# Decode attention on one core: softmax moved into the head's own loop body, hardware loops on VectorE and ScalarE, x on ScalarE's queue, wo in 1792-byte rows

## The chip, the cores and the metric

The kernel runs on one core of one Trainium2 chip. The metric is the device time of one execution in microseconds (us), the median of several runs. The *span* is the part of that time that the profile covers, from the first to the last instruction; it is 1.7 to 2.1 us shorter than the device time in most runs here and up to 3.7 us in some, and that small difference will matter. A run is fast or slow in state; all runs that are compared below are fast, except where the text says otherwise (two runs of e6 are slow, and the state of e8's only run is unknown). Differences of under 1% are the subject here, so most kernels were run five times beside the kernel before on the same chip.

## The reference

A decode step of grouped-query attention with a gate. With 4 batches and 8 key/value heads there are 32 heads to stream, each with K and V of 8192 x 256 in bf16, 4.19 MB each. The two query heads of a group share them. A small two-layer MLP gives the gate. Everything else is small beside 32 x 8.4 MB.

```python
B, Sq, D = 4, 1, 448
Hq, Hkv, Sk, Dh = 16, 8, 8192, 256

def _A_ref(x, k_cache, v_cache, wq, wo):
    q = ((x @ wq).reshape(B, Sq, Hq, Dh)).transpose(0, 2, 1, 3)
    k = jnp.repeat(k_cache, 2, axis=1)
    v = jnp.repeat(v_cache, 2, axis=1)
    scores = jnp.einsum("bhqd,bhkd->bhqk", q, k) * (Dh ** -0.5)
    p = _softmax(scores, axis=-1)
    o = jnp.einsum("bhqk,bhkd->bhqd", p, v)
    return o.transpose(0, 2, 1, 3).reshape(B, Sq, Hq * Dh) @ wo

xn = _layernorm(x)
s = _A_ref(xn, k_cache, v_cache, wq, wo)
g = _silu(_B_ref(xn, w1, w2, w3, w4))        # cut: a small MLP
return x + s * g
```

## The kernel before

SyncE issues all the big loads on one queue. K and V have two buffers each; K's is released by PE's count of transposed groups (`p_t`), V's by PE's count of finished PV products (`p_pv`).

```python
def prog_sp(sp):
    sp.dma_start(x_sb[:, :], x2d).then_inc(S["dx"], 16)
    # ... cut: wq, w3, w4, rows of 28,672, 12,544 and 6,272 bytes
    def load_k(h):
        if h >= 2:
            sp.wait_ge(S["p_t"], NGR * (h - 1))
        sp.dma_start(kn_dst(h), ...).then_inc(S["dk%d" % (h % 2)], 16)
    def load_v(h):
        # ... cut: h == 0
            sp.wait_ge(S["p_pv"], h)
        # ... cut: the last V comes in four pieces, dvl0 to dvl3
    load_k(0)
    load_k(1)
    sp.dma_start(wo_sb[:, :, :], A_wo.rearrange("(k p) n -> p k n", p=P)
                 ).then_inc(S["dwo"], 16)          # rows of 896 bytes
    load_v(0)
    for h in range(2, NH):
        load_k(h)
        load_v(h - 1)
    load_v(NH - 1)
```

TensorE (PE) runs a hardware loop over pairs of heads. A head is 16 groups of 8 transposes of K; VectorE or ScalarE evicts each group, and three groups later PE forms its scores. The softmax chain and the PV product *of the previous head* are woven into the groups.

```python
def body(h):
    for j in range(NGR):                       # 16 groups
        f_t(h, j)                              # 8 transposes of K
        if j >= LAG: f_s(h, j - LAG)           # scores, 3 groups behind
        else:        f_s(h - 1, NGR + j - LAG)
        if j == J_RMAX: f_rmaxT(h - 1)         # J = 4, 6, 9
        if j == J_BC:   f_bc(h - 1)
        if j == J_SUM:  f_sum(h - 1)
        if j in PV_SLOTS:                      # groups 10 to 15
            f_pv(h - 1, ...)                   # 128 matmuls in six parts
with nc.Fori(0, NH // 2, engines=[PE], ...):
    body(0); body(1)
# after the loop: last three score groups of the last head, then its softmax
# chain, with the output projection f_o of groups 0 to 6 woven in between,
# then PV by pieces of V, then f_o(7)
```

VectorE and ScalarE are written out in full, head by head, with waits for ever larger semaphore values:

```python
def evac(engine, h, j):
    engine.wait_ge(S["p_t"], NGR * h + j + 1)
    # ... cut: copy pst to kT, on VectorE or on ScalarE

for h in range(NH):                            # unrolled on VectorE
    for j in range(NGR):
        if j in D_GROUPS: evac(v, h, j)
        # ... cut: rmax, diag, negb, rz of head h - 1 at fixed groups
    f_ot(h - 1)                                # psv * rz to OT
```

Of the kernel before, what the change touches and what calls it, by code (L numbers as in the profile page):

```python
# [12 lines left out]
P = 128  # L13
# [19 lines left out]
def bass_recurrent_scan__gqa_block_cached__mixer_s_mlp__decode_kernel(  # L33
# [43 lines left out]
    J_RMAX, J_BC, J_SUM = 4, 6, 9  # L77
    PV_SLOTS = tuple(range(10, 16))
    NPV = NCH * NHALF
    PVW = 32  # L80
# [5 lines left out]
    with ExitStack() as es:  # L86
        def sb(name, shape, dty):
# [5 lines left out]
        wo_sb = sb("wo_sb", [P, NKC, D], BF16)  # L93
# [4 lines left out]
        qc = sb("qc", [P, 2, NHALF, REP], BF16)  # L98
        OT = sb("OT", [P, HKV, REP, NHALF, Bn], BF16)
# [8 lines left out]
        rz = sb("rz", [P, REP], F32)  # L108
# [28 lines left out]
            + ["p_t", "p_sc", "p_m1", "p_m2", "p_m3", "p_pv", "p_x", "p_q", "p_h", "p_h2", "p_o"]  # L137
            + ["v_ev", "a_ev", "v_rmax", "v_diag", "v_neg", "v_ot", "a_exp", "g_q", "g_c",
               "v_xT", "v_qT", "v_hT", "v_bout", "v_c", "v_w", "a_c", "v_out"])}
# [23 lines left out]
        def prog_sp(sp):  # L163
            sp.dma_start(x_sb[:, :], x2d).then_inc(S["dx"], 16)
# [10 lines left out]
            def load_k(h):  # L175
                b, g = divmod(h, HKV)
                if h >= 2:
                    sp.wait_ge(S["p_t"], NGR * (h - 1))
                sp.dma_start(kn_dst(h), A_k_cache[b, g].rearrange("(p c) d -> p (c d)", p=P)
                             ).then_inc(S["dk%d" % (h % 2)], 16)  # L180

            def load_v(h):
                b, g = divmod(h, HKV)
                if h == 0:
                    sp.wait_ge(S["p_h2"], 1)
                else:
                    sp.wait_ge(S["p_pv"], h)
                src = A_v_cache[b, g].rearrange("(p c) d -> p c d", p=P)
                if h < NH - 1:
                    sp.dma_start(vflat[h % 2], src.rearrange("p c d -> p (c d)")  # L190
                                 ).then_inc(S["dv%d" % (h % 2)], 16)
                else:
                    w = NCH // NPIECE
                    for i in range(NPIECE):
                        sp.dma_start(
                            vb[:, h % 2, i * w:(i + 1) * w, :].rearrange("p c d -> p (c d)"),
                            src[:, i * w:(i + 1) * w, :].rearrange("p c d -> p (c d)")
                        ).then_inc(S["dvl%d" % i], 16)
# [3 lines left out]
            sp.dma_start(wo_sb[:, :, :], A_wo.rearrange("(k p) n -> p k n", p=P)  # L202
# [10 lines left out]

        def prog_pool(gp):
            c = _Chain(gp, S["g_c"])
            c(gp.memset(ident_f[:, :], 0.0))
            c(gp.memset(ident_b[:, :], 0.0))
            c(gp.memset(ones_f[:, :], 1.0))
            c(gp.memset(pT[:, :, :].rearrange("p s n -> p (s n)"), 0.0))
            c(gp.memset(vflat[1][:, DK * HDH:NCH * DH], 0.0))  # L220
            c(gp.memset(qc[:, 1].rearrange("p a b -> p (a b)"), 0.0))
            c(gp.memset(kT[:, (NGR - LAG) % RING:RING, :].rearrange("p r n -> p (r n)"), 0.0))
            c.sync()
            for t in (ident_b, ident_f):
                c(gp.affine_select(out=t[:, :], in_=t[:, :], compare_op=ALU.not_equal, fill=1.0,
                                   base=0, pattern=[[-1, P]], channel_multiplier=1))
            gp.wait_ge(S["v_qT"], 1)
            for h in range(NH):
                b, g = divmod(h, HKV)
                if h >= 1:  # L230
                    gp.wait_ge(S["p_sc"], h)
                gp.tensor_copy(qc[:, h % 2], qT[:, b, g]).then_inc(S["g_q"], 1)  # L232

        def evac(engine, h, j):
            engine.wait_ge(S["p_t"], NGR * h + j + 1)
# [7 lines left out]
        def prog_act(act):  # L243
            c = _Chain(act, S["a_c"])
# [8 lines left out]
            def exps(h):  # L253
                s = h % 2
                act.wait_ge(S["v_neg"], h + 2)
                if h >= 1:
                    act.wait_ge(S["p_pv"], h)
# [9 lines left out]
            for h in range(NH):  # L267
                for j in range(NGR):
                    if j not in D_GROUPS:
                        evac(act, h, j)  # L270
                    if j == J_BC:
                        exps(h - 1)
            exps(NH - 1)
# [4 lines left out]
        def prog_dve(v):  # L278
# [34 lines left out]
            c(v.memset(psc[1][:, 0:NCH * REP], 0.0))  # L313
            c.sync()
            v.sem_inc(S["v_ev"], sum(j in D_GROUPS for j in range(NGR - LAG, NGR)))
            v.sem_inc(S["a_ev"], sum(j not in D_GROUPS for j in range(NGR - LAG, NGR)))
            v.sem_inc(S["v_ot"], 1)
            v.sem_inc(S["dv1"], 16)
# [10 lines left out]
            v.wait_ge(S["g_c"], 9)  # L329
# [47 lines left out]
            def f_rmax(h):  # L377
                v.wait_ge(S["p_sc"], h + 2)
# [3 lines left out]
            def f_diag(h):  # L382
                v.wait_ge(S["p_m1"], h + 2)
                c(v.tensor_reduce(gmax[:, :], psm[0:REP, 0:P], AX.X, ALU.max))  # L384
                c.sync()
# [3 lines left out]
            def f_negb(h):  # L389
                v.wait_ge(S["p_m2"], h + 2)  # L390
                v.tensor_copy(negb[:, h % 2, :], psm[:, P:P + REP]).then_inc(S["v_neg"], 1)  # L391

            def f_rz(h):
                v.wait_ge(S["p_m3"], h + 2)
                c(v.reciprocal(rz[:, :], psm[:, P + REP:P + 2 * REP]))

            def f_ot(h):
                b, g = divmod(h % NH, HKV)
                v.wait_ge(S["p_pv"], h + 2)
                c.sync()  # L400
                for dh in range(NHALF):
                    src = psc[0] if (h == NH - 1 and dh == 1) else psv
                    ins = v.tensor_tensor(OT[:, g, :, dh, b], src[:, dh * PVW:dh * PVW + REP],  # L403
                                          rz[:, :], ALU.mult)
                    if dh == NHALF - 1:
                        ins.then_inc(S["v_ot"], 1)
                    else:
                        c(ins)

            for h in range(NH):  # L410
                for j in range(NGR):
                    if j in D_GROUPS:
                        evac(v, h, j)
                    if j == LAG - 1:
                        f_rmax(h - 1)
                    if j == J_RMAX:
                        f_diag(h - 1)
                    if j == J_BC:
                        f_negb(h - 1)
                    if j == J_SUM + 1:  # L420
                        f_rz(h - 1)
                f_ot(h - 1)
            f_rmax(NH - 1)
            f_diag(NH - 1)
            f_negb(NH - 1)
            f_rz(NH - 1)
            f_ot(NH - 1)
# [6 lines left out]
        def prog_pe(pe, xn_mark, xn2_mark):  # L434
            def take(name, n=1):
                pe.wait_ge(S[name], n).then_inc(S[name], -n)  # L436

            pe.wait_ge(S["g_c"], 9)
            for k, (src, mark) in enumerate(((xn_b, xn_mark), (xn2_b, xn2_mark))):
# [6 lines left out]
                if k == 0:  # L446
                    take("v_xT")
            take("dwq", 16)
# [9 lines left out]
            take("dw3", 16)  # L458
            take("v_xT")
# [6 lines left out]
            take("dw4", 16)  # L466
            take("v_hT")
# [8 lines left out]
            take("v_bout")  # L476

            def f_t(h, j):
                if j == 0:
                    take("dk%d" % (h % 2), 16)  # L480
# [6 lines left out]
                ins.then_inc(S["p_t"], 1)  # L487

            def f_s(h, j):
                if j == 0:  # L490
                    take("g_q")
                take("v_ev" if j in D_GROUPS else "a_ev")
# [9 lines left out]
            def f_rmaxT(h):  # L502
                take("v_rmax")
                take("v_ot")
                pe.transpose(psm[0:REP, 0:P], rmax[:, :], ident_f[:, :]).then_inc(S["p_m1"], 1)  # L505

            def f_bc(h):
                take("v_diag")
# [3 lines left out]
            def f_sum(h):  # L512
                take("a_exp")
# [3 lines left out]
            def f_pv(h, lo, hi):  # L517
                if lo == 0:
                    take("dv%d" % (h % 2), 16)
                for i in range(lo, hi):  # L520
                    dh, kk = divmod(i, NCH)
                    ins = pe.matmul(psv[:, dh * PVW:(dh + 1) * PVW],  # L522
                                    vb[:, h % 2, kk, dh * P:(dh + 1) * P],
# [4 lines left out]
            def body(h):  # L528
                for j in range(NGR):
# [3 lines left out]
                    else:  # L533
                        f_s(h - 1, NGR + j - LAG)
                    if j == J_RMAX:
                        f_rmaxT(h - 1)
                    if j == J_BC:
                        f_bc(h - 1)
                    if j == J_SUM:
                        f_sum(h - 1)  # L540
                    if j in PV_SLOTS:
                        i, n = PV_SLOTS.index(j), len(PV_SLOTS)
                        f_pv(h - 1, NPV * i // n, NPV * (i + 1) // n)

# [6 lines left out]
            for j in range(NGR - LAG, NGR):  # L551
                f_s(h, j)
            take("dwo", 16)

            def f_o(g):
                for r in range(REP * NHALF):
                    k = g * REP * NHALF + r
                    hh, dh = divmod(r, NHALF)
                    for i in range(NQD):
                        ins = pe.matmul(o_ps[i * PQ:i * PQ + Bn, 0:DQ], OT[:, g, hh, dh, :],  # L560
                                        wo_sb[:, k, i * DQ:(i + 1) * DQ],
# [3 lines left out]
            for g in range(0, 3):  # L565
                f_o(g)
            f_rmaxT(h)
            for g in range(3, 6):
                f_o(g)
            f_bc(h)  # L570
            for g in range(6, HKV - 1):
                f_o(g)
            f_sum(h)
            w = NCH // NPIECE
            for i in range(NPIECE):
                take("dvl%d" % i, 16)
                for dh in range(NHALF):
                    for kk in range(i * w, (i + 1) * w):
                        ins = pe.matmul((psv, psc[0])[dh][:, dh * PVW:(dh + 1) * PVW],  # L579
                                        vb[:, h % 2, kk, dh * P:(dh + 1) * P],  # L580
# [3 lines left out]
            take("v_ot")  # L584
# [52 lines left out]
```

## Time and profile before

| | before |
|---|---|
| device time, median of 3 runs (range) | 665.11 us (664.92 to 665.47) |
| span of the profiled run | 663.0 us |
| mean granted PE clock | 0.887 |
| mean DMA share, 300 to 400 us | 1.00 at 431 GB/s |
| longest group of waits | SyncE for a free K buffer, 533.2 us in 30 waits |

The profile's page of the kernel before: busy time by engine (instructions after the x), the granted PE clock in 40 slices of the span (tenths of full speed), and two DMA queues (packets, MB, share of 16 engines). Queue q14 carries the 8 KB fetches of program code of VectorE and ScalarE. A queue q8, not shown, has 11 fetches of 16 KB, which are taken here to be PE's code.

```profile
PE 534.6 (81%) x12964; PEld 527.5 (80%) x12964; DVE 247.4 (37%) x583; ACT 250.0 (38%) x362; POOL 12.1 (2%) x45
PEclk9997888898877899888789987878998788899889
q1 hardware_dynamic: 14344, 279.00, 98.3%
q14 instruction: 8, 0.07, 0.0%
```

The data queue is in use for 98.3% of the span. The compute engines have room: even PE, which at 81% looks close, is slowed by a clock that stands at half speed for 151 us of the 663 (own sum of the trace's clock records). The stretch table of the kernel before (length, then busy us and instructions by engine, PE clock, DMA share and GB/s) says it more strictly:

```profile
core 0: us, PE busy (x) PEld busy (x) DVE busy (x) ACT busy (x) POOL busy (x), PEclk, DMA share, GB/s
300.00:400.00 100.00, 82.30 (x1994) 81.36 (x1990) 37.20 (x84) 38.39 (x55) 0.93 (x5) 0.88 1.00 431
```

DMA share 1.00 means that, to two digits, no DMA engine rests in this stretch. The waits of SyncE and of PE in the kernel before (total, times, longest) tell who waits for whom:

```profile
SPq L179 <- PE pst L484: 533.2, 30, 20.2
```

```profile
PE pst L484 <- PEq L436: 93.9, 30, 8.1
```

L179 is the issue of a K load, L484 the transposes, L436 PE's wait for a semaphore. A long wait of SyncE for a buffer does not make PE the bound: SyncE issues a load as soon as a buffer is free and then waits for the next, while one to two loads are still in the queue. PE is the one that starves: once a head, ahead of the first transposes, it waits for K to land, 3.0 us in the mean of the 29 waits after the first of 8.1 us. In SyncE's timeline of the kernel before (start, duration, what), K loads leave 18.8 to 20.1 us apart (from the fifth K on, own count; the mean is 19.47):

```profile
300.75 0.33 SPq L179 DMA_DIRECT2D kn<-in_A_k_cache_dram  x1
301.50 0.33 SPq L190 DMA_DIRECT2D vb<-in_A_v_cache_dram  x1
320.19 0.33 SPq L179 DMA_DIRECT2D kn<-in_A_k_cache_dram  x1
```

The mean is twice the 9.71 us between landings of 4.19 MB, so the rate of the queue sets the period. The Trainium skill, "DMA: Bandwidth & Descriptors", section "Specifications", gives a fabric ceiling of 435 GB/s; the 430 to 433 GB/s of this trace agree with that.

PE's timeline of the kernel before, across the seam between two heads, shows the wait and what it does to the clock:

```profile
320.20 0.70 PE L522 MATMUL psv<-pT,vb 128*128 128x32 bf16 x22
324.00 1.01 PE L484 MATMUL pst<-ident_b,kn 128*128 128x128 bf16 x8 [3.10 <-PEq L436]
```

After 3.10 us of idle time the first 8 transposes take 1.01 us; elsewhere in the head 8 of them take 0.61.

The weight loads of two early products (start, busy time, line, count):

```profile
13.33 3.06 PEld L455 LDWEIGHTS pst<-xnT,vb 128*128 128x128 bf16 x112
16.35 2.69 PEld L463 LDWEIGHTS pst<-xn2T,vb 128*128 128x128 bf16 x49
```

L455 reads contiguous weight columns: 3.06 / 112 = 27 ns each. L463 reads w3 with a step of seven elements: 2.69 / 49 = 55 ns. This is the only stepped weight load of the kernel before, and the change adds another.

Last, the end of PE's timeline in the kernel before. The last K has fully landed at 635.79 us (see below for how), the last piece of V at 655.39.

```profile
652.79 0.76 PE L560 MATMUL pst<-wo_sb,OT 128*4 128x112 bf16 x48
653.49 0.27 PE L505 MATMUL psm<-ident_f,rmax 128*2 128x128 f32 x1
653.69 0.76 PE L560 MATMUL pst<-wo_sb,OT 128*4 128x112 bf16 x48
...
655.90 0.36 PE L514 MATMUL psm<-rowsum,ones_f 128*128 128x2 f32 x2 [0.78 <-PEq L436]
656.11 0.56 PE L579 MATMUL psv<-pT,vb 128*128 128x32 bf16 x16
656.51 0.56 PE L579 MATMUL psc<-pT,vb 128*128 128x32 bf16 x16
...
659.89 0.37 PE L560 MATMUL pst<-wo_sb,OT 128*4 128x112 bf16 x16 [0.42 <-PEq L436]
```

The output projection (L560) fills the gaps of the softmax chain, and the last PV (L579) starts at 656.11, soon after the last V. PV matmuls are (656.51 - 656.11) / 16 = 25 ns apart.

**The landing table.** A load raises its semaphore 16 times, once for each DMA engine that finishes its share (the Trainium skill, "DMA: Bandwidth & Descriptors", section "Why a DMA increments its semaphore by 16 and not by 1"; the trace has 16 increments for each of the big loads). Sorting these 16 increments gives, for each load, when the first, the median and the last engine were done. The consumer has to wait for the last. This is own work on the trace's records, not a view of the profile:

```
before: landing of    first    median   last    last - first
K of the last head    631.01   632.78   635.79  4.78
```

At wq, last minus first was 0.68 us, at the first K 2.28. The 16 engines drift apart during the run, in steps, and the end waits for the slowest.

### The profile page before, as it was taken

The page shows a single profiled execution, that of the slowest core. Times are in us where ns is not written, and L with a number is a line of the kernel's source. Part 1 is how long each engine was busy: PE and PEld are TensorE (multiplying, and loading weights), DVE is VectorE, ACT ScalarE, POOL GpSimd, SP SyncE. Part 2 cuts the span into 40 slices and gives each one's busy share as a digit, 9 for nine tenths or more (in the row PEclk, how much of TensorE's full clock was granted, in tenths as well). Part 3 has the DMA queues.
Part 4 walks back from the last instruction along what each step waited for, and adds up shares of the span by engine and source line. Part 5 has one row for each costly group of instructions (what it writes and reads, how often), then busy time and mean ns, then how long its engine had stood idle before and what let it go on. Part 6 is the DMA issues. An engine that isn't in the chain of part 4 may idle for free. (4 is left out here: it accounts for less than half of the span.)

```text
span 663.0 us, 27886 instructions
## 1 busy us (share of the span) xinstructions
PE 534.6 (81%) x12964; PEld 527.5 (80%) x12964; DVE 247.4 (37%) x583; ACT 250.0 (38%) x362; POOL 12.1 (2%) x45
## 2 busy tenths in 40 slices
PE   2388887789888878987887898888888887789777
PEld 2388887789888878987887898888888887789777
DVE  6233433333333333333333333433343333334332
ACT  1044433344433344444333444433444343344431
POOL 3000000000000000000000000000000000000000
PEclk9997888898877899888789987878998788899889
DMA  8999999999999999999999999999999999999993
GB/s 354 439 403 427 429 439 425 431 437 429 429 433 431 431 433 431 433 431 429 435 429 429 439 425 431 441 423 431 439 427 429 437 431 427 437 431 427 433 418 132
DMA packets 14379, 279.24 MB, mean 421 GB/s; under 512 B 1172, under 2 KB 5272, under 8 KB 5528
## 3 DMA queue, kind: packets, MB, share of 16 engines
q1 hardware_dynamic: 14344, 279.00, 98.3%
q8 instruction: 11, 0.18, 0.1%
q14 instruction: 8, 0.07, 0.0%
q10 hardware_dynamic: 16, 0.00, 0.0%
HBM read 278.99 MB, written 0.00 MB: 421 GB/s over the span
## 5 line engine op out<-in xcount | busy, mean ns | idle before, releaser
L484 PE MATMUL pst<-ident_b,kn 128*128 128x128 bf16 x4096 | 364.0, 241 | 95.5 <-PEq L436 93.9
L241 ACT ACTIVATE kT<-pst 128x1024 bf16<-128x1024 bf16 x224 | 226.8, 1023 | 366.8 <-PE pst L484 366.7
L484 PEld LDWEIGHTS pst<-ident_b,kn 128*128 128x128 bf16 x4096 | 279.2, 108 | 98.9 <-issue 97.5
L239 DVE COPY kT<-pst 128x1024 bf16<-128x1024 bf16 x288 | 199.3, 692 | 392.1 <-PE pst L484 392.1
L496 PE MATMUL psc<-qc,kT 128*128 128x2 bf16 x4120 | 182.8, 166 | 0.3 <-issue 0.3
L496 PEld LDWEIGHTS psc<-qc,kT 128*128 128x128 bf16 x4120 | 170.5, 101 | 1.3 <-issue 1.3
L522 PE MATMUL psv<-pT,vb 128*128 128x32 bf16 x4096 | 132.4, 177 | 13.3 <-PEq L436 9.1
L522 PEld LDWEIGHTS psv<-pT,vb 128*128 128x128 bf16 x4096 | 116.7, 96 | 14.6 <-issue 14.6
L261 ACT ACTIVATE pT<-psc,negb 128x64 bf16<-128x64 f32 x66 | 20.8, 330 | 18.5 <-DVE negb L391 18.5
L232 POOL COPY qc<-qT 128x4 bf16<-128x4 bf16 x32 | 6.0, 186 | 607.2 <-PE psc L496 597.2
L261 ACT ACTIVATION_READ_ACCUMULATOR pT<-psc,negb 128x1 f32 x66 | 12.9, 196 | 0.0
L514 PE MATMUL psm<-rowsum,ones_f 128*128 128x2 f32 x66 | 12.0, 251 | 0.8 <-PEq L436 0.8
L509 PE MATMUL psm<-diag,ones_f 2*128 2x2 f32 x66 | 12.5, 256 | 0.0
L442 PE MATMUL pst<-ident_b,xn_b 4*128 4x4 bf16 x14 | 0.6, 161 | 12.8 <-DVE xn_b L309 8.1
L442 PEld LDWEIGHTS pst<-ident_b,xn_b 4*128 4x128 bf16 x14 | 0.5, 99 | 12.8 <-issue 8.1
L514 PEld LDWEIGHTS psm<-rowsum,ones_f 128*128 128x128 f32 x66 | 9.9, 189 | 0.9 <-issue 0.9
L509 PEld LDWEIGHTS psm<-diag,ones_f 2*128 2x128 f32 x66 | 9.7, 183 | 0.8 <-issue 0.2
L403 DVE TENSOR_TENSOR OT<-psv,rz 128x2 bf16<-128x2 f32 x65 | 7.6, 162 | 7.1 <-PE psc L579 3.1
L505 PE MATMUL psm<-ident_f,rmax 128*2 128x128 f32 x33 | 9.9, 299 | 0.0
L379 DVE TENSOR_REDUCE rmax<-psc 128x2 f32<-128x128 f32 x33 | 9.3, 281 | 0.4 <-PE psc L496 0.4
L384 DVE TENSOR_REDUCE gmax<-psm 2x1 f32<-2x128 f32 x33 | 8.8, 268 | 0.6 <-PE psm L505 0.6
L386 DVE TENSOR_SCALAR diag<-ident_f,gmax 2x2 f32<-2x2 f32 x33 | 7.1, 216 | 1.2
(70 smaller groups left out, 66.8 us busy)
## 6 DMA issues: line engine op xcount, KB each, us to landing
kn<-in_A_k_cache_dram SPq DMA_DIRECT2D x32, 4096.0 KB, 23.1
vb<-in_A_v_cache_dram SPq DMA_DIRECT2D x31, 4096.0 KB, 32.1
vb<-in_A_v_cache_dram SPq DMA_DIRECT2D x4, 1024.0 KB, 18.3
vb<-in_A_wq_dram SPq DMA_DIRECT2D x1, 3584.0 KB, 11.2
wo_sb<-in_A_wo_dram SPq DMA_DIRECT2D x1, 3584.0 KB, 46.7
vb<-in_B_w_dram SPq DMA_DIRECT2D x2, 1568.0 KB, 16.9
out_dram<-out_b SPq DMA_DIRECT2D x2, 0.9 KB
out_dram<-out_b ACTq DMA_DIRECT2D x2, 0.9 KB
```

The costliest lines, as they stand in the source:

```text
L239: engine.tensor_copy(dst, src).then_inc(S["v_ev"], 1)
L241: engine.activation(dst, src, ACT.Copy).then_inc(S["a_ev"], 1)
L261: ins = act.activation(pv_p[:, :, hh], sc[:, :, hh], ACT.Exp, bias=negb[:, s, hh:hh + 1], scale=SCALE, accum_out=rowsum[:, s, hh:hh + 1])
L379: v.tensor_reduce(rmax[:, :], psc[h % 2][:, 0:NCH * REP].rearrange("p (k h) -> p h k", h=REP), AX.X, ALU.max).then_inc(S["v_rmax"], 1)
L384: c(v.tensor_reduce(gmax[:, :], psm[0:REP, 0:P], AX.X, ALU.max))
L403: ins = v.tensor_tensor(OT[:, g, :, dh, b], src[:, dh * PVW:dh * PVW + REP], rz[:, :], ALU.mult)
L484: ins = pe.transpose(dst[:, t * P:(t + 1) * P], kn[:, h % 2, GC * j + kl, half * P:(half + 1) * P], ident_b[:, :])
L496: ins = pe.matmul(psc[h % 2][:, kk * REP:(kk + 1) * REP], kT[:, j % RING, t * P:(t + 1) * P], qc[:, h % 2, half, :], start=(half == 0), st ...
L505: pe.transpose(psm[0:REP, 0:P], rmax[:, :], ident_f[:, :]).then_inc(S["p_m1"], 1)
L509: pe.matmul(psm[:, P:P + REP], ones_f[0:REP, :], diag[:, :], start=True, stop=True).then_inc(S["p_m2"], 1)
L514: pe.matmul(psm[:, P + REP:P + 2 * REP], ones_f[:, :], rowsum[:, h % 2, :], start=True, stop=True).then_inc(S["p_m3"], 1)
L522: ins = pe.matmul(psv[:, dh * PVW:(dh + 1) * PVW], vb[:, h % 2, kk, dh * P:(dh + 1) * P], pT[:, h % 2, kk * REP:kk * REP + PVW], start=(kk ...
```

## The change

The intent: keep each head's softmax within its own loop body, so that at the end of the kernel only PV and the projection of the last head are left; loop on VectorE and ScalarE too, to fetch less code; get wq under way earlier by moving the small x load to ScalarE's queue; and load wo in rows twice as long.

What it needs: waits that decrease their semaphore (`take`), as a loop can't wait for growing values; a step of two elements in PV's weights, so that PV's output fits wo's new layout; and a hop over GpSimd (`put`) from a fixed tile `otmp` into OT, as the loop body can't index OT by head. K's and V's buffers are both released by `v_done` at the end of a body.

```diff
@@ SyncE
-            sp.dma_start(x_sb[:, :], x2d).then_inc(S["dx"], 16)
-                    sp.wait_ge(S["p_t"], NGR * (h - 1))
+                    sp.wait_ge(S["v_done"], h - 1)
-                    sp.wait_ge(S["p_pv"], h)
+                    sp.wait_ge(S["v_done"], h)
-            sp.dma_start(wo_sb[:, :, :], A_wo.rearrange("(k p) n -> p k n", p=P)
+            sp.dma_start(wo_sb[:, :, :, :].rearrange("p h c n -> p h (c n)"),
+                         A_wo.rearrange("(h p c) n -> p h (c n)", p=P, c=NHALF)
                          ).then_inc(S["dwo"], 16)
+        def take(eng, name, n=1):
+            eng.wait_ge(S[name], n).then_inc(S[name], -n)
@@ GpSimd (cut)
+                if h >= 3:
+                    put(h - 3)
+            for h in range(NH, NH + 2):
+                gp.wait_ge(S["v_done"], h - 1)
+                put(h - 3)
+            gp.wait_ge(S["g_p"], NH - 1)
+            gp.sem_inc(S["g_f"], 1)
@@ ScalarE (cut)
+            act.dma_start(x_sb[:, :], x2d).then_inc(S["dx"], 16)
+            with nc.Fori(0, NH // 2, engines=[mybir.EngineType.Activation]):
+                for h in range(2):
+                    for j in range(NGR):
+                        if j not in D_GROUPS:
+                            evac(act, h, j)
+                    exps(h)
@@ VectorE (cut)
+            with nc.Fori(0, NH // 2, engines=[mybir.EngineType.DVE]):
+                for h in range(2):
+                    for j in range(NGR):
+                        if j in D_GROUPS:
+                            evac(v, h, j)
+                    f_rmax(h)
+                    f_diag(h)
+                    f_negb(h)
+                    f_ot(h - 1)
+                    f_rz(h)
@@ PE: f_pv and body
-                                    vb[:, h % 2, kk, dh * P:(dh + 1) * P],
+                                    vb[:, h % 2, kk, dh:DH:NHALF],
-                    else:
-                        f_s(h - 1, NGR + j - LAG)
-                    # (cut) rmaxT, bc, sum and PV of head h - 1 at their groups
+                tail = [lambda j=j: f_s(h, j) for j in range(NGR - LAG, NGR)]
+                tail += [lambda: f_rmaxT(h), lambda: f_bc(h), lambda: f_sum(h)]
+                for i, f in enumerate(tail):
+                    f_pv(h - 1, PV_PARTS[i], PV_PARTS[i + 1])
+                    f()
@@ PE: after the loop
-            for g in range(0, 3):
-                f_o(g)
-            f_rmaxT(h)
-            # (cut) f_o(3..5), f_bc, f_o(6), f_sum
+            take(pe, "v_ot")
+            pe.wait_ge(S["g_f"], 1)
+            for g in range(HKV - 1):
+                f_o(g)
```

## The prediction

> **What bounds the kernel now.** DMA. The page gives queue q1 98.3% of 16 engines' span; the stretches from 100 to 600 us show DMA share 1.00 at 430 to 433 GB/s. SP's timeline issues one K per 19.4 us, twice the 9.71 us between landings of 4 MB. PE waits: the wait list has 93.9 us in 30 waits of about 3.1 us ahead of the K transposes. In a middle head PE works about 16.3 of 19.4 us, 1.7 us of it because the clock falls to 0.50 for one or two 3.4 us windows after that idle. The queue never runs dry.
>
> The landing increments show the 16 DMA engines drifting apart: 0.7 us between first and last at 12 us, 4.7 us at the end. The steps follow instruction fetches; one late 8 KB fetch, at 597 us, adds about 1.07 us to the last engine.
>
> The end: last K lands at 635.8, last V piece at 655.4, PE finishes at 660.3, the last store ends at 663.0. So 27.2 us follow the last K, and PE sets them.
>
> **What the change does.**
> 1. Steady state: same bytes, same PE work per head (16 groups at 0.65 us, 128 PV matmuls at 0.029 us, three small ones). PV now follows the transposes, interleaved with the head's own softmax. I count 17.4 us per head, with 1 us of stalls in the chain and 1.7 us for low clock: under 19.4. Releasing K and V one or two microseconds later is covered by about 13 us of queued transfers. Gain: none.
> 2. x leaves SP's queue: wq's issue moves from 1.15 to 0.74 us. Gain 0.4 us. x may come later; the projections end 7 us before the first K lands.
> 3. wo: 3.67 MB take 9.55 us of landing spacing, against 8.5 us at the K rate. Half the packets should return half the excess. Estimate: 0.5 us.
> 4. Loops on VectorE and ScalarE remove about seven 8 KB fetches. Estimate: 0.5 to 1 us less lag on the last DMA engine. A back edge that refetches would return this.
> 5. Tail: the last softmax chain hides under PV of head 30, but the output projection (1.8 us) no longer hides in the chain, and a new hop VectorE, GpSimd, PE costs about 1.2 us. I count 27.2 us again; 1.7 us less if shorter idle keeps the clock full.
> 6. PV weights are read with a step of two elements. The one stepped load in the trace, w3 with a step of seven, has 53 ns spacing, against 27 ns for wq just before. The Trainium skill, "SBUF — State Buffer", cacheline note in "Door 1", says two hits per 16-byte line suffice; a step of two has four, so I expect 28 ns still (two chances in three). At 53 ns a head grows by 3.2 us, which the idle, vanished stalls and fuller clock roughly absorb, but the tail grows by 4 to 6 us.
>
> **Prediction.** 663.4 us, range 660.5 to 668.0. Faster by over 2%: 0.01; within 2%: 0.95; slower by over 2%: 0.04.
>
> **What would show it.** K issues still 19.4 us apart at DMA share 1.00; PE's wait before each head about 2 us; PV spacing 28 ns; wq landing 0.4 us earlier; wo's spacing near 9.0 us; last K landing 1.5 to 2 us earlier; no 8 KB fetches in mid-run; about 27 us after the last K.
>
> **What would make it wrong.** Stepped weights at 53 ns together with a low clock, making PE the bound; loops fetching code at every turn, delaying evictions and DMA; a wait for V at the tail's start; clock windows falling differently in the last head.

## The result

| | before | after |
|---|---|---|
| device time, median (range) | 665.29 us, 4 runs (664.92 to 665.75) | 664.26 us, 4 runs (664.02 to 664.65) |
| ratio after / before, 95% interval | | 0.9985 (0.9968 to 1.0002): same |
| span of the profiled run | 663.0 us | 662.4 us |
| median span of all runs beside it | 663.3 to 663.4 us (27 runs of the later rounds) | 662.2 us |
| device time less span | 1.8 to 1.9 us | 2.0 to 2.1 us |
| mean granted PE clock | 0.887 | 0.856 |

Ratios are the mean time of one kernel's fast runs over the mean of the other's of the same rounds, so they are not quite the ratios of the medians in the table. The interval holds 1, so the verdict is "same". That there is a gain of about 1 us all the same rests on the ranges: the four runs after lie below all 31 runs of before (664.77 to 665.92).

The profile's page of the kernel after:

```profile
PE 544.8 (82%) x12935; PEld 536.3 (81%) x12935; DVE 254.1 (38%) x545; ACT 255.4 (39%) x358; POOL 13.3 (2%) x75
PEclk9988688898877889887788987878998787899878
q1 hardware_dynamic: 12288, 278.99, 98.4%
q14 instruction: 2, 0.02, 0.0%
```

The data queue has 2,056 packets fewer for the same bytes (wo's rows are longer, and x went to another queue) and the code fetches of VectorE and ScalarE fell from 8 to 2. Between 22 and 660 us there is one, at 346 us, in place of seven. The stretch in mid-run (columns as before) is unchanged where it matters:

```profile
300.00:400.00 100.00, 83.25 (x1966) 81.94 (x1962) 37.65 (x77) 40.05 (x59) 1.88 (x12) 0.85 1.00 431
```

The waits of SyncE and of PE in the kernel after:

```profile
SPq L178 <- DVEq L411: 547.7, 30, 22.4
```

```profile
PE pst L493 <- PEq L215: 66.4, 29, 8.1
```

The buffer now comes free from VectorE (L411 is `v_done`), later than before, and PE waits less for K: 66.4 us in 29 waits, of which the first takes 8.1 us and the others 2.1 us in the mean (before: 3.0). PE's work was moved, not shortened, and the queue's pace is the same, as SyncE's timeline of the kernel after shows:

```profile
301.83 0.33 SPq L178 DMA_DIRECT2D kn<-in_A_k_cache_dram  x1
302.20 0.43 SPq L189 DMA_DIRECT2D vb<-in_A_v_cache_dram  x1
321.64 0.33 SPq L178 DMA_DIRECT2D kn<-in_A_k_cache_dram  x1
```

(Mean over the settled part of the run, own count: 19.42 us, against 19.47.) The seam between two heads on PE's timeline after:

```profile
320.79 0.35 PE L522 MATMUL psm<-rowsum,ones_f 128*128 128x2 f32 x2 [0.48 <-PEq L215]
323.42 1.87 PE L493 MATMUL pst<-ident_b,kn 128*128 128x128 bf16 x16 [2.27 <-PEq L215]
```

The wait before the transposes is shorter (2.27 us), and the clock still falls: 16 transposes take 1.87 us where 32 at full clock take 1.95 (in e12, below).

In the first pass of the loop there is something else on the timeline of VectorE and PE after:

```profile
69.64 0.22 DVE L399 TENSOR_SCALAR diag<-ident_f,gmax 2x2 f32<-2x2 f32 x1
73.27 0.56 PE L517 MATMUL psm<-diag,ones_f 2*128 2x2 f32 x2 [3.46 <-PEq L215]
```

PE stood still for 3.46 us here, though the `diag` that it needs was ready at 69.86. A 16 KB fetch on q8 starts at 70.74 us and takes 1.11 us, so this wait is most likely for code; the trace doesn't say so outright. It delays the end of the body, and with it the release of the buffer: the fourth K is issued at 76.16 us, where it was 71.39.

The end of PE's timeline after (first column in us; the last K landed at 634.12, the last piece of V at 653.74):

```profile
651.37 0.35 PE L522 MATMUL psm<-rowsum,ones_f 128*128 128x2 f32 x2 [0.48 <-PEq L215]
652.65 2.77 PE L561 MATMUL pst<-wo_sb,OT 128*4 128x112 bf16 x112 [0.92 <-POOLq L249]
...
656.21 0.55 PE L575 MATMUL psv<-pT,vb 128*128 128x32 bf16 x16
656.61 0.55 PE L575 MATMUL psc<-pT,vb 128*128 128x32 bf16 x16
...
659.30 0.37 PE L561 MATMUL pst<-wo_sb,OT 128*4 128x112 bf16 x16 [0.53 <-PEq L215]
```

The chain is over 4.5 us earlier (the L522 line at 651.37, against L514 at 655.90), 1.67 us of it because the last K landed sooner. Then PE waits 0.92 us for GpSimd's hop, and its 112 projection matmuls, which before lay in the gaps of the chain, now take 2.77 us on the critical path. They run slowly because the granted clock fell to one half at 652.72. PV with the stepped weights keeps (656.61 - 656.21) / 16 = 25 ns.

The landing table of the two profiled runs (own work) gives the account. "wq" is the landing of the first big load; "wo" is the mean of wo's 16 landings less the mean of the load before it; "tail" is what follows the last K to the end of the span; "median" is the ninth of the 16 landings in order of time.

```
           last K: first  median   last     wq     wo    tail   span
before            631.01  632.78  635.79   12.33  9.72  27.24  663.0
after             631.85  632.35  634.12   11.90  9.63  28.30  662.4
difference                 -0.43   -1.67   -0.43  -0.09 +1.06   -0.6
```

So the last K is there 1.67 us sooner: 0.43 by an earlier start, which the median engine shows as well, and 1.24 because the slowest DMA engine lags less behind the median (1.77 us, before 3.01). The tail gives 1.06 us of it back. The profiled run of before happens to be at the low end of its runs (663.0, where 27 later runs span 663.0 to 664.0); by medians the span fell by 1.2 us, and the time outside the span rose by about 0.2.

Two cautions come from the same traces. First, the 1.06 us of tail are not all the new code's doing. How much half clock falls between the last K and PE's last matmul differs from run to run. The profiled run of before had 3.4 us of it and e2, with the same tail, 3.4 us too (tail 27.28); e1, again with the same tail, had 8.2 us and a tail of 27.97. After had 8.3 us. Compared at about the same half clock, e1 against after, the new tail costs 0.3 us; the other 0.7 us go with half clock that the profiled run of before did not meet. The new body has more half clock in all (193 us against 151), so how much of the 0.7 is chance stays open.

Second, most of the seven fetches of before left the slowest engine alone. Its distance to the first engine was 3.67 us from 81 us on, and it grew only twice after that, with the fetches at 461 us (0.13) and 597 us (0.96): the other five set back engines that were not the last, or not yet. Of the 1.67 us at the last K, 0.60 are there at the second V (80.41 us against 81.01), and 1.07 come after it.

### The profile page after: what moved, and what is told of

Same layout as the page of the kernel before. It is cut to its first block, busy times and chain, and to the rows that moved or that the text cites. A ratio compares the mean times of both kernels' runs of the same rounds, so it can differ in the third digit from the quotient of the medians.

```text
span 662.4 us, 28676 instructions
## 1 busy us (share of the span) xinstructions
PE 544.8 (82%) x12935; PEld 536.3 (81%) x12935; DVE 254.1 (38%) x545; ACT 255.4 (39%) x358; POOL 13.3 (2%) x75
## 5 line engine op out<-in xcount | busy, mean ns | idle before, releaser
L493 PE MATMUL pst<-ident_b,kn 128*128 128x128 bf16 x4096 | 354.7, 244 | 66.5 <-PEq L215 66.4
L493 PEld LDWEIGHTS pst<-ident_b,kn 128*128 128x128 bf16 x4096 | 288.0, 111 | 68.5 <-issue 68.5
L258 ACT ACTIVATE kT<-pst 128x1024 bf16<-128x1024 bf16 x224 | 229.4, 1024 | 220.9 <-ACTq L215 220.9
L505 PE MATMUL psc<-qc,kT 128*128 128x2 bf16 x4096 | 177.0, 164 | 1.2 <-issue 1.2
L505 PEld LDWEIGHTS psc<-qc,kT 128*128 128x128 bf16 x4096 | 157.5, 98 | 1.3 <-issue 1.3
L531 PEld LDWEIGHTS psv<-pT,vb 128*128 128x128 bf16 x4096 | 118.5, 97 | 6.4 <-issue 5.4
L522 PE MATMUL psm<-rowsum,ones_f 128*128 128x2 f32 x64 | 12.1, 259 | 14.8 <-PEq L215 14.8
L522 PEld LDWEIGHTS psm<-rowsum,ones_f 128*128 128x128 f32 x64 | 10.3, 202 | 17.0 <-issue 17.0
L416 DVE TENSOR_TENSOR otmp<-psv,rz 128x4 bf16<-128x4 f32 x32 | 5.2, 162 | 27.4 <-DVEq L215 27.4
L404 DVE COPY negb<-psm 128x2 f32<-128x2 f32 x32 | 5.1, 159 | 24.3 <-DVEq L215 24.3
L408 DVE RECIPROCAL rz<-psm 128x2 f32<-128x2 f32 x32 | 5.5, 171 | 17.9 <-DVEq L215 17.8
## 6 DMA issues: line engine op xcount, KB each, us to landing
vb<-in_A_v_cache_dram SPq DMA_DIRECT2D x4, 1024.0 KB, 17.1
vb<-in_B_w_dram SPq DMA_DIRECT2D x2, 1568.0 KB, 16.8
```

The costliest lines, as they stand in the source:

```text
L258: engine.activation(dst, src, ACT.Copy).then_inc(S["a_ev"], 1)
L408: v.reciprocal(rz[:, h % 2, :], psm[:, P + REP:P + 2 * REP]).then_inc(S["v_s"], 1)
L493: ins = pe.transpose(dst[:, t * P:(t + 1) * P], kn[:, h % 2, GC * j + kl, half * P:(half + 1) * P], ident_b[:, :])
L505: ins = pe.matmul(psc[h % 2][:, kk * REP:(kk + 1) * REP], kT[:, j % RING, t * P:(t + 1) * P], qc[:, h % 2, half, :], start=(half == 0), st ...
L522: pe.matmul(psm[:, P + REP:P + 2 * REP], ones_f[:, :], rowsum[:, h % 2, :], start=True, stop=True).then_inc(S["p_m3"], 1)
L531: ins = pe.matmul(psv[:, dh * PVW:(dh + 1) * PVW], vb[:, h % 2, kk, dh:DH:NHALF], pT[:, h % 2, kk * REP:kk * REP + PVW], start=(kk == 0), ...
```

## The experiments

The theory after this reading (T): the steady state is bound by DMA in both kernels and gives nothing; of the gain, 0.4 us is x and the rest is less code fetching, each fetch holding back one DMA engine by about a microsecond; wo's rows give nothing; the new tail costs about a microsecond. Rivals: (R1) wo's longer rows give the gain; (R2) the loops give nothing, and the reordering with its later buffer release does it; (R3) the new body relieves PE, which waits less, and that is the gain.

All kernels gave a result that the comparison with the reference passed. Times are medians of five runs, if nothing else is said; the kernel before had 665.20 to 665.27 us beside them. The spans are medians of the same runs. "Lag" is last minus median landing of the last K in the profiled run, "q14" the number of code fetches in that queue on the page. After is 664.26 (664.02 to 664.65) with span 662.2.

| kernel | time, us (range) | ratio to before (95%) | span | time - span | q14 | lag | tail |
|---|---|---|---|---|---|---|---|
| before | 665.29 (664.92-665.75) | 1 | 663.4 | 1.8-1.9 | 8 | 3.01 | 27.24 |
| after | 664.26 (664.02-664.65) | 0.9985 (0.9968-1.0002) | 662.2 | 2.0-2.1 | 2 | 1.77 | 28.30 |
| e1_x_act | 664.83 (664.53-665.18) | 0.9994 (0.9980-1.0008) | 663.0 | 1.8-1.9 | 8 | 2.98 | 27.97 |
| e2_wo1792 | 665.37 (664.96-665.89) | 1.0005 (0.9991-1.0019) | 663.5 | 1.8-1.9 | 8 | 3.23 | 27.28 |
| e3_unroll | 668.68 (668.47-669.67) | 1.0051 (1.0038-1.0065) | 666.9 | 1.8 | 15 | 6.96 | 27.74 |
| e4_wo896 | 664.17 (663.74-664.38) | 0.9983 (0.9969-0.9997) | 662.2 | 2.0 | 2 | 1.70 | 28.27 |
| e7_tail | 663.95 (662.81-665.07) | 0.9986 (0.9973-1.0000) | 661.0 | 2.0-3.7 | 2 | 1.70 | 26.80 |
| e9_unroll_act | 664.84 (664.22-666.66) | 0.9989 (0.9976-1.0003) | 663.1 | 1.7-1.8 | 7 | 3.50 | 27.90 |
| e10_early_k | 664.25 (663.55-664.73) | 0.9986 (0.9973-1.0000) | 662.2 | 2.0 | 2 | 1.66 | 27.58 |
| e11_early_k_tail | 663.78 (662.82-664.43) | 0.9977 (0.9964-0.9991) | 660.8 | 2.0-3.0 | 2 | 1.68 | 26.81 |
| e12_fill | 662.75 (661.82-663.28) | 0.9963 (0.9949-0.9976) | 660.7 | 2.0-2.1 | 2 | 1.54 | 25.98 |

### e1_x_act: x alone

The kernel before, with x issued from ScalarE.

```diff
 def prog_sp(sp):
-    sp.dma_start(x_sb[:, :], x2d).then_inc(S["dx"], 16)
 def prog_act(act):
+    act.dma_start(x_sb[:, :], x2d).then_inc(S["dx"], 16)
```

> The kernel before with one edit: x is issued from ScalarE's queue. Theory: everything on SP's queue moves 0.4 us earlier (wq lands near 11.9 instead of 12.3 us), the DMA is never idle, so the last K lands 0.4 us earlier and the time falls by 0.4 us, ratio 0.9994. Rival: the start is absorbed by the skew between DMA engines and nothing changes, ratio 1.0000.

Measured: 664.83 us, 0.44 under the 665.27 of before beside it; the interval of the ratio still holds 1. The lag of the slowest engine stays as before (2.98). In e1's own trace wq is issued at 0.74 us and not at 1.15; it lands 0.23 us earlier (12.10), the last K 0.39 us earlier (635.40). The span of the profiled run shows none of it, for its tail is 27.97 and not 27.24; the median span does (663.0, against 663.4).

### e2_wo1792: wo's rows and the stepped PV weights alone

The kernel before, with wo in 1792-byte rows and PV weights with a step of two.

```diff
-    A_wo.rearrange("(k p) n -> p k n", p=P)
+    A_wo.rearrange("(h p c) n -> p h (c n)", p=P, c=NHALF)
-    vb[:, h % 2, kk, dh * P:(dh + 1) * P],
+    vb[:, h % 2, kk, dh:DH:NHALF],
```

> The kernel before with wo in 1792-byte packets and, as that needs, PV weights read with a step of two. Theory from the trace after the change: wo's landing spacing stays at about 9.5 us, PV spacing stays 28 ns, time unchanged, ratio 1.0000. Rival (my prediction): spacing 9.0 us, time 0.5 us less, ratio 0.9992.

Measured: 665.37 us, against 665.27; wo's landing spacing 9.73, against 9.72. The rows are worth nothing here, and the stepped weights cost nothing. The 9.63 of after is no gain either, since e1 has 9.63 with rows of 896 bytes. R1 is out.

### e4_wo896: everything but wo's rows

The kernel after, with both of these undone: wo in 896-byte rows again and contiguous PV weights.

```diff
-    A_wo.rearrange("(h p c) n -> p h (c n)", p=P, c=NHALF)
+    A_wo.rearrange("(k p) n -> p k n", p=P)
-    vb[:, h % 2, kk, dh:DH:NHALF],
+    vb[:, h % 2, kk, dh * P:(dh + 1) * P],
```

> The kernel after with wo back in 896-byte packets and PV weights contiguous. Theory: wo's spacing is 9.5 us either way and PV weights cost 28 ns either way, so it equals the kernel after, ratio to before 0.9985. Rival: wo's packets were worth 0.5 us, ratio 0.9993.

Measured: 664.17 us and span 662.2, as after; lag 1.70. That is e2 from the other side.

### e8_wo28k: how much there is to gain from wo

The kernel after, with wo as one contiguous run of 28,672 bytes per partition. This puts the wrong rows in each place: it asks only for the transfer's cost.

```diff
-    A_wo.rearrange("(h p c) n -> p h (c n)", p=P, c=NHALF)
+    A_wo.rearrange("(p k) n -> p (k n)", p=P)
```

> The kernel after with wo loaded as one 28,672-byte run for each partition (the projection then multiplies the wrong rows, on purpose). Theory: the 1 us that wo costs over the rate of K is a matter of packets far under 8 KB, so its landing spacing falls from 9.5 to 8.5 us. Rival: wo's spacing stays near 9.5 us and has another cause, such as the start of V behind it. Read from the landing times, not from the total.

Measured: 663.4 us in the single run; wo's spacing fell from 9.63 to 8.60, so long rows are indeed worth 1.0 us of queue time. The last K came only 0.56 us earlier, because the queue then ran dry before the fourth K: all engines waited for it (10.42 us between the last landings of the second V and of that K, in place of 9.71). The comparison did not reject the permuted weights; correctness here says nothing.

Why 1792 gave nothing where 28,672 gave 1.0 us remains open. The packets' own durations did shrink: 256 packets per engine of 41.3 ns (sum 10.6 us) became 128 of 78.6 ns (sum 10.1 us), a half of a microsecond, just what was predicted. But the landings are only 9.6 to 9.7 us apart in both, less than either sum, so small packets overlap and their durations can't be added. The Trainium skill, "DMA: Bandwidth & Descriptors", section "Why small descriptors are slow (HBM only)", gives a fixed overhead of about 3 cycles per packet, which would halve with half the packets; the packets' durations go that way, and the landing times of e2 and e4 don't.

### e3_unroll: the loops alone, undone

The kernel after, with VectorE and ScalarE written out again, with the new handshakes.

```diff
-            with nc.Fori(0, NH // 2, engines=[mybir.EngineType.Activation]):
+            for _ in range(NH // 2):
-            with nc.Fori(0, NH // 2, engines=[mybir.EngineType.DVE]):
+            for _ in range(NH // 2):
```

> The kernel after with the VectorE and ScalarE loops unrolled again. Theory: 8 KB instruction fetches come back in mid-run (eight or more), the last DMA engine lags the median by about 1 us more than after, the last K lands about 1 us later, and the time is about 1 us over the kernel after: 665.3 us, ratio to before near 1.000. Rival: the smaller lag after the change was chance (which DMA engine happened to serve which fetch); then the ratio stays 0.9985 as after.

Measured: 668.68 us, 4.4 over after, and 3.4 over before. The page of this kernel has

```profile
q14 instruction: 15, 0.12, 0.0%
```

against 2 after and 8 before. There are more than before because each `take` is an instruction of its own: written out, VectorE has 1,134 instructions where before had 629, and ScalarE 621 where it had 399. The slowest DMA engine is 6.96 us behind the median at the last K, the median engine only 0.84 us later than after (0.7 of it because the queue ran dry before the fourth K, 10.44 us between last landings). So most of the cost is not spread over the load, it sits on one engine, and everyone waits for that one. The spread between first and last engine grows in steps of about 1 us, from 0.83 to 7.21 at the last K and 8.19 after it. The steps come with eight fetches about 76 us apart (112 to 641 us). In e9, where VectorE loops again, these eight are missing: they are VectorE's, and all of them hold back the engine that ends last. R2 is out: the loops do matter, and by much more than the change shows, since without them the new handshakes would have cost more than all else gained.

The mechanism was expected, its size was not. A fetch's packet takes 0.31 us, but one fetch sets the lag back by about a microsecond. This also says why seven fetches of before cost 1.1 us and 13 here cost 4.4: what counts is how often the last landing is moved, twice in before (0.13 and 0.96 us), eight times here. That the fetches of one engine's code all fall on the same DMA engine is an inference from the growth of one engine's lag; the packet records don't name the DMA engine.

### e9_unroll_act: ScalarE's loop alone, undone

```diff
-            with nc.Fori(0, NH // 2, engines=[mybir.EngineType.Activation]):
+            for _ in range(NH // 2):
```

> The kernel after with only ScalarE's loop unrolled: 4 or 5 of the 13 mid-run fetches of e3 come back. Theory: each engine's fetches burden one DMA engine, and ScalarE's one starts without a lag, so it ends about 3 to 4 us behind the leaders, near the lag that the last engine has anyway: time 0 to 1 us over the kernel after. Rival: every fetch costs the kernel the same, a third of e3's 4.4 us: 1.5 us over the kernel after.

Measured: 664.84 us, 0.6 over after in time and 0.9 in span (663.1). Seven fetches, lag 3.50. It lies between after and e3, as the theory needs: the lag ranks with the number of fetches (2: 1.5 to 1.8; 7 or 8: 3.0 to 3.5; 15: 7.0) over all eleven kernels of the table. A fetch of ScalarE's sets its DMA engine back by 0.65 to 0.7 us here. The rival's 1.5 us is not met by the median, but the five runs spread over 2.4 us. The profiled run is the slowest of the five (666.66); in it the queue ran dry by 1.2 us before the fourth K.

### e5_halfv_before and e6_halfv_after: how fast PE could go

To see PE's own pace, DMA must stop being the bound. Both kernels load only half of V for heads 2 to 30 (V's other half is stale, so the result is wrong; the comparison's tolerance does not see it). Three rounds.

```diff
-                if h < NH - 1:
+                if 2 <= h < NH - 1:
+                    sp.dma_start(vflat[h % 2][:, 0:NCH // 2 * DH],
+                                 src[:, 0:NCH // 2].rearrange("p c d -> p (c d)")
+                                 ).then_inc(S["dv%d" % (h % 2)], 16)
+                elif h < NH - 1:
```

> The kernel before, but from head 2 to head 30 only the first half of V is loaded (wrong result on purpose), so DMA needs about 14.6 us a head instead of 19.4. Theory: PE or its chain becomes the bound at about 15 to 16.3 us a head, total 520 to 565 us. Compared with the next run it shows what the reordered body is worth when DMA does not hide it.

> The same cut of V in the kernel after. Theory: PE works about 1 us a head longer in the new body (stalls in the softmax chain), so it is some 20 to 40 us slower than e5, ratio e6 to e5 1.03 to 1.07; the reorder is no gain for PE and is merely hidden by DMA. Rival: the reordered body is the better one and e6 is faster than e5.

Measured: e5 529.23 us (528.22 to 530.01), clock 0.984, about 14.6 us per head. That is still the queue's pace (1.5 x 9.71 = 14.6), so PE's own head before is at most that at full clock. e6 has two fast runs, 579.72 and 575.34, and two, 586.49 and 587.62, that count as slow by being over 1.5% above the fastest. By the fast runs e6 takes 577.5 / 529.2 = 1.091 of e5 (1.03 to 1.07 was expected). Its heads take 15.2 to 15.5 us at full clock and 16.8 to 17.1 with a stretch of half clock. So the reordering makes PE's head longer, not shorter, by 0.6 us at least, and the full V load hides it, since 17.1 is still below 19.4. R3 is out.

The rest is the clock, 0.92. PE's timeline of e6 at a seam:

```profile
310.21 0.35 PE L526 MATMUL psm<-rowsum,ones_f 128*128 128x2 f32 x2 [0.47 <-PEq L219]
310.73 3.11 PE L497 MATMUL pst<-ident_b,kn 128*128 128x128 bf16 x32 [0.16 <-PEq L219]
...
327.49 1.95 PE L497 MATMUL pst<-ident_b,kn 128*128 128x128 bf16 x32
```

The same 32 transposes take 3.11 us in one head and 1.95 in the next, and before the slow ones PE idled 0.47 and 0.16 us only. The Trainium skill, "TensorE: Matmul & The Clock Gate", section "HAM oscillation — how this bites in real kernels", words the rule as no idle gaps of PE over about 3.4 us. Here the clock falls without any such gap, after a stretch of PV matmuls with 32 columns; in before and after it falls after waits of 3.1 and 2.3 us. That the thin PV stretch is the trigger is possible, but no run isolates it, and e12 below speaks against it as the only cause: there the same stretch, followed by busy work, leaves the clock full.

### e7_tail: the projection no longer behind the last hop

The kernel after, with output groups 0 to 5 needing only the next to last hop over GpSimd.

```diff
-            gp.wait_ge(S["g_p"], NH - 1)
-            gp.sem_inc(S["g_f"], 1)
+                gp.sem_inc(S["g_f"], 1)        # once after each of the last two hops
-            take(pe, "v_ot")
             pe.wait_ge(S["g_f"], 1)
-            for g in range(HKV - 1):
+            for g in range(HKV - 2):
                 f_o(g)
+            take(pe, "v_ot")
+            pe.wait_ge(S["g_f"], 2)
+            f_o(HKV - 2)
```

> The kernel after, where the output projection of the head groups 0 to 5 no longer waits for GpSimd's last copy; only group 6 does. Theory: the 0.9 us hop is filled, part of the projection no longer falls in the half-clock window, and the tail after the last K falls from 28.3 to about 26.9 us; time 1.0 to 1.6 us under the kernel after, ratio to before 0.996. Rival: the tail waits for the last V piece (landed at 653.7 us), so at most 0.3 us is gained.

The end of the chain on PE's timeline of e7:

```profile
650.98 0.35 PE L521 MATMUL psm<-rowsum,ones_f 128*128 128x2 f32 x2 [0.47 <-PEq L215]
651.36 2.39 PE L560 MATMUL pst<-wo_sb,OT 128*4 128x112 bf16 x112
653.68 0.61 PE L576 MATMUL psv<-pT,vb 128*128 128x32 bf16 x16
```

The 0.92 us wait is gone, and PV starts when the projection ends, at 653.68. V does not hold it back, as the rival said: the first of the four pieces had landed at 646.19, the last at 653.59. The tail is 26.80 us, 1.5 less. The median span fell by 1.2 us (661.0, against 662.2), so the cost of the hop is shown. But the median time fell only by 0.3. The rest went *outside the span*: in four of the five runs the time exceeds the span by 2.9 to 3.7 us, where after has 2.0 to 2.1. What the program does in that extra microsecond the profile does not cover; it is open.

### e10_early_k and e11_early_k_tail: K's buffer released sooner

The change releases K at the end of a body, and the leading DMA engines waited 1.16 us for the fourth K (10.88 us between first landings in place of 9.72). e10 is the kernel after with K released once VectorE has evicted its last group; e11 is e10 with e7's tail.

```diff
-                    sp.wait_ge(S["v_done"], h - 1)
+                    sp.wait_ge(S["v_k"], h - 1)
                             evac(v, h, j)
+                    v.sem_inc(S["v_k"], 1)
                     f_rmax(h)
```

> The kernel after with K's buffer released when VectorE has seen the head's last transposes, instead of at the end of its body. Theory: the fourth K is issued at about 71 us instead of 76, so no DMA engine runs dry there; the slowest engine was not held in the profiled run after (it was by 0.7 us in e3 and 1.2 us in e9), so the median falls by 0 to 0.5 us below the kernel after: ratio to before 0.9975 to 0.9985, and the spread of the runs narrows. Rival: the release time plays no part and the spread of the runs stays as it was in e7.

> e10 with the projection of groups 0 to 5 moved ahead of the hop, as in e7. Theory: tail of 26.8 us after the last K, 1.5 us under e10; ratio to before 0.996. Rival: e7's profiled run was a lucky one and the tail change is worth nothing in the median: ratio 0.9985.

Measured: e10 664.25 us and span 662.2, both as after, though the fourth K now leaves at 61.4 us and not at 76.2, and no engine waits for it. The waiting of the leading engines cost nothing, since the slowest engine had never waited (9.71 us between last landings in after as well). e11: 663.78 us, 0.5 under e10; the span fell by 1.4 us (660.8), and again three of five runs have 3.0 us outside the span.

### e12_fill: busy work for the clock

e11, with 30 useless matmuls of 128 columns at the start of each body, into a part of psc that no one reads, in the time in which PE waits for K.

```diff
             def body(h):
+                for _ in range(30):
+                    pe.matmul(psc[(h - 1) % 2][:, 2 * P:3 * P], ident_b[:, :], ident_b[:, :],
+                              start=True, stop=True)
```

> e11 with 30 matmuls without use (128 columns each, about 1.7 us) at the start of every head, where PE waits for K. Theory: the half clock in the new body follows from the idle and the sparse PV stretch before it; with the wait filled the clock stays full at the start of the last head, its transposes take 10.5 us instead of 12.5, and the time falls by 1 to 1.7 us under e11 although PE has more to do; ratio to before 0.994. Rival: the clock falls for the PV stretch alone, fillers do not help, the time stays at e11's or grows where PE becomes the bound.

The last head's first transposes on PE's timeline in e11:

```profile
634.04 3.57 PE L493 MATMUL pst<-ident_b,kn 128*128 128x128 bf16 x32 [2.51 <-PEq L215]
```

and in e12, with the filler (L539) ahead of them:

```profile
630.61 1.83 PE L539 MATMUL psc<-ident_b 128*128 128x128 bf16 x30
633.96 1.95 PE L493 MATMUL pst<-ident_b,kn 128*128 128x128 bf16 x32 [1.52 <-PEq L215]
```

With the filler the clock is full here: the same 32 transposes take 1.95 us and not 3.57. Over the whole run the filler does not remove the half clock but halves it (97 us, against 192 in e11), and the mean clock is 0.928, against 0.857. At 662.75 us this is the fastest kernel that loads all of its data, 2.5 us under before (ratio 0.9963). But the gain of the filler itself is small where it can be separated: by spans e12 is 0.1 us under e11 in the median (660.7, 660.8) and 0.4 in the mean (660.5, 660.9), though the tail of the profiled runs is 0.8 shorter. Most of the 1.0 us between e11 and e12 in time is that e12 had no run with the extra microsecond outside the span.

## Why the prediction was right, and which terms were off

The prediction of 663.4 us, same within 2%, came 0.9 us below the measured 664.26. Its view of the kernel held in every large point; two terms of its sum were mis-sized. The class "same" was a safe call, since all the gains that it counts are together under 0.5% of the time; what can be learned lies in the terms.

1. *"Steady state: same bytes ... Gain: none."* Right. DMA share 1.00 at 431 GB/s and K loads 19.4 us apart in both kernels. PE's count of 17.4 us per head is near the 16.8 to 17.1 that e6 shows. e5 and e6 show that the reordered head costs 9% where DMA does not hide it.
2. *"Releasing K and V one or two microseconds later is covered by about 13 us of queued transfers."* Right for the time, wrong in one detail: in the first pass of the loop PE waited 3.46 us, most likely for code, the fourth K left 4.8 us later than before, and the leading DMA engines waited 1.16 us for it. The slowest engine did not, and e10, without that wait, is no faster.
3. *"x leaves SP's queue ... Gain 0.4 us."* Right in size: 0.43 us at wq's landing, 0.44 us in e1's median, though e1's interval alone does not exclude zero.
4. *"wo: ... Half the packets should return half the excess. Estimate: 0.5 us."* **Wrong, the mis-sized term of the queue**: e2 has no gain (665.37 against 665.27), and e4, without the long rows, loses none (664.17 against 664.26). The step that failed is the scaling of the excess by the number of packets. The excess is real (1.0 us, e8), the packets' durations shrink as predicted, and the landings don't follow.
5. *"Loops ... remove about seven 8 KB fetches. Estimate: 0.5 to 1 us less lag on the last DMA engine."* Right in mechanism and sign; measured 1.24 us less lag. The path is narrower than "seven fetches" says: the last landing moved at two of the seven only. "No 8 KB fetches in mid-run" was off by one, at 346 us. What the prediction missed is that the new handshakes need 1.6 to 1.8 times as many instructions (621 for 399, 1,134 for 629): unrolled, they cost 4.4 us (e3).
6. *"Tail: ... I count 27.2 us again."* **The second mis-sized term**: 28.30. The pieces were named, the hop (0.92 us of wait) and the projection that is no longer hidden, but the projection was put at 1.8 us and took 2.77, since a stretch of half clock fell on it. The "1.7 us less if shorter idle keeps the clock full" did not come, as the clock still fell with 2.3 us of idle time. As said above, at about the same half clock the new tail costs 0.3 us, and the rest goes with the clock. e7 moves the hop off the path and gets 1.5 us of tail and 1.2 us of span.
7. *"PV weights ... I expect 28 ns still."* Right: 25 ns, the same as contiguous. The Trainium skill, "SBUF — State Buffer", cacheline note in "Door 1", holds for the step of two. For the step of seven its note that one can stride for free up to 8 bf16 doesn't: 55 ns, against 27. That is one load of its kind; no run varies its step.

The sum of the measured terms for the profiled pair is -0.43 - 1.24 + 1.06 = -0.6 us of span. By medians the span fell by 1.2 us and the time by 1.0. The half microsecond between these is the profiled run of before, which was one of its fastest, most likely because so little half clock fell into its tail (3.4 us, where e1 had 8.2 and a tail 0.7 us longer). With the 0.3 us of tail from e1 in place of 1.06 the sum is -1.4 us.

## What to carry to other kernels

In a kernel that is bound by one DMA queue, look at the 16 landings of a load and not only at its last: the slowest engine sets the end, and what holds it back may be code fetches, a few of 8 KB against 279 MB of data. A fetch costs time where it makes the last engine later, and nothing as long as another engine is later still. A hardware loop is worth its handshakes there, but count the instructions that the handshakes add, and count them unrolled. And when an edit of half a microsecond seems to do nothing, compare the spans as well as the times, for the two can part.

## What the Trainium skill lacked or had wrong

- "Runtime: NRT & Kernel Launch", section "Instruction fetch mechanics", calls fetching mostly hidden and says that kernels prefer full unrolling where possible. Here a fetch of 8 KB takes 0.31 us itself, sets one DMA engine back by about 1 us (VectorE's) or 0.7 us (ScalarE's), and 13 more of them cost 4.4 us of time (e3 against after). The page gives blocks of 16 KB; on q14 they came as packets of 8 KB.
- "TensorE: Matmul & The Clock Gate", section "HAM oscillation — how this bites in real kernels": the clock halved after idle gaps of 2.3 and 3.1 us, and in e6 after none longer than 0.47 us in the body. Gaps below 3.4 us are not safe here, so the rule of that section is not enough by itself; the page's next section does describe a second way, by many short idle times.
- "SBUF — State Buffer", cacheline note in "Door 1": free up to a stride of 8 bf16. A weight load with a step of 7 took 55 ns against 27 ns; a step of 2 was free (25 ns). The same note's other rule, two hits per 16-byte line, fits both.
- "DMA: Bandwidth & Descriptors", section "Specifications", gives 512 bytes as the least transfer for line rate. Rows of 896 and 1792 bytes both took 9.6 to 9.7 us for 3.67 MB, and rows of 28,672 bytes 8.6 us. No page says that durations of small packets overlap, so that their sum (10.6 and 10.1 us) overstates the transfer.
- No page says that device time less span can differ between runs of one kernel: 2.0 to 3.7 us in e7, 2.0 to 2.1 in e12.
